# Windowed attention and channel mix: q and k of seven batches turned on VectorE instead of TensorE

## The chip, the cores and the metric

One core of a Trainium2 chip runs the whole program. Its engines run side by side, each through its own list of instructions in order: PE (TensorE: matmuls, and PEld for the weight loads), DVE (VectorE), ACT (ScalarE), POOL (GpSimd, which here mainly issues the loads) and SP (SyncE, which issues the stores). They wait for each other by semaphores. The metric is the device time of one execution in microseconds; the kernel before takes 245.48 us, the median of 3 runs from 244.85 to 245.68.

## The reference

```python
B, H, S, D = 8, 8, 576, 64                       # attention
scores = (q @ k.T) / sqrt(D)
rel = pos[:, None] - pos[None, :]
bias = slopes[h] * -abs(rel)                     # slopes: 2 ** -(h + 1)
scores = where((rel >= 0) & (rel < 128), scores + bias, -1e9)
attn_out = softmax(scores) @ v                   # per batch and head
x = attn_out as (B, S, 512)                      # channel mix
x_prev = x shifted down by one token, zero first
xk = mu_k * x + (1 - mu_k) * x_prev
xr = mu_r * x + (1 - mu_r) * x_prev
out = sigmoid(xr @ w_r) * (relu(xk @ w_k) ** 2 @ w_v)
```

The weights are 512x1024, 1024x512 and 512x512. Inputs and the output are float32; the kernel computes in bf16 with float32 sums.

## The kernel before, in words

**Pairs and units.** The attention runs over 32 pairs: pair `it` is batch b = it // 4 and the two heads 2g and 2g+1 with g = it % 4. A token attends to at most 128 tokens up to itself, so its keys lie in its own block of 128 tokens or in the one before: 576 tokens are four blocks and a tail of 64. The channel mix runs over two batches at a time (P = 0 to 3, 1152 tokens), cut into units of 256, 384 or 512 tokens.

**One pair, in order.** POOL loads q and k with a cast to bf16 (`load_ql`, lines 105 to 109: four heads of one of q and k for the first 512 tokens, four tokens on each of 128 partitions) and the tail of 64 tokens apart (`load_tail`, line 100). DVE gathers two heads by token (`by_token`, line 126, tile `ct`); PE turns them with eight transposes by the identity (`qk_transp`, line 135), so that the 64 numbers of a head lie on partitions, as the contraction of the scores wants it; ACT copies the result out of PSUM (`qk_copy`, line 115). Once in a batch PE turns the tails (`tail_transp`, line 148) and DVE copies them (lines 154 and 155). PE computes the scores in two halves of six matmuls with 64 rows each, the two heads side by side in the array (`scores`, line 187); ACT takes the exponential (line 195); DVE multiplies with the mask that holds bias and window (line 200); PE multiplies with v (`av`, line 218), where a column of ones gives the sums; DVE divides (`norm`, lines 229 and 230); PE turns the result (`x_transp`, line 238); ACT copies it to `xt` (line 243), channels on partitions.

**Mixing.** `mix` computes on DVE dl = x - x_prev (line 263) and then xk = mu_k dl + x_prev and xr = mu_r dl + x_prev (line 270), each in one instruction with the factor of the channel.

**Channel mix.** For a unit PE computes xk @ w_k in eight parts (`mm1`, line 281), ACT takes the relu (line 287), DVE squares it (`square`, line 292, tile `kk`), PE computes xr @ w_r (`mm3`, line 300), ACT the gate (line 306), PE the product with w_v in two halves (`mm2`, line 315), DVE multiplies with the gate (`product`, line 321), and SP stores the result (line 324).

**What sets the order.** A table `ORDER` fixes every engine's list (PE, ACT, DVE, POOL), and `plan` issues the operations by it. Names in it are an operation with its indices: `score.4.0` is the first half of the scores of pair 4, `m1.0.256.3` part 3 of `mm1` in the unit of P = 0 that begins at token 256, `kk`, `m3`, `m2a`, `m2` and `oo` belong to the same units. PSUM is shared by rings: two double banks `sa` (scores and av), one bank `tp` (transposes) and three banks `mm`. A matmul into a ring waits until the reader of the bank's last content is done.

Of the kernel before, what the change touches and what calls it, by code (L numbers as in the profile page):

```python
# [16 lines left out]
def kernel(  # L17
# [12 lines left out]
    nc = tc.nc  # L30
# [31 lines left out]
    p_tp = ctx.enter_context(tc.tile_pool(name="p_tp", bufs=1, space=bass.MemoryType.PSUM))  # L62
    p_mm = ctx.enter_context(tc.tile_pool(name="p_mm", bufs=3, space=bass.MemoryType.PSUM))
# [4 lines left out]
    ldr = cst.tile([128, 2, NHW, 2, NF * D], FP32, name="ldr")  # L68
    qk_buf = [cst.tile([128, 2, SM], BF16, name=f"qk{i}") for i in range(NBUF)]
    vs_buf = [cst.tile([128, NF, H, W], BF16, name=f"vs{i}") for i in range(NLD)]  # L70
    ql_buf = [cst.tile([128, 2, 2, H // 2, NF * D], BF16, name=f"ql{i}") for i in range(2)]
    ts_buf = [cst.tile([128, H, D], BF16, name=f"ts{i}") for i in range(NLD)]
    at_buf = [cst.tile([128, 2 * 1024 + 64], BF16, name=f"at{i}") for i in range(NAT)]

    tt_buf = [cst.tile([128, G, 3, 64], BF16, name=f"tt{i}") for i in range(2)]
    tv_buf = [cst.tile([128, H, W], BF16, name=f"tv{i}") for i in range(NLD)]
    xt_buf = [cst.tile([128, NPO, 2 + S], BF16, name=f"xt{i}") for i in range(2)]
# [22 lines left out]
    def load_tail(b, i):  # L100
        nc.gpsimd.dma_start(
            out=ts_buf[b % NLD][64 * i:64 * i + 64],
            in_=(q, k)[i][b, :, SM:S, :].rearrange("h p d -> p h d"))
# [40 lines left out]
    def tail_transp(b):  # L144
        ts = ts_buf[b % NLD]
# [6 lines left out]
    def tail_copy(b):  # L152
        t4 = T.pop(("tt", b))[:, 0:128 * G].rearrange("p (g t c) -> p g t c", g=G, t=2)
        nc.vector.tensor_copy(out=tt_buf[b % 2][:, :, 2], in_=t4[:, :, 0])
        nc.vector.tensor_copy(out=tt_buf[b % 2][:, :, 0], in_=t4[:, :, 1])
# [10 lines left out]
    def scores(it, e):  # L166
        early = it < NEARLY
        b, g = divmod(it, G)
        qk, tt = qk_buf[it % NBUF], tt_buf[b % 2]
# [19 lines left out]

    def at_half(it, e):  # L190
# [3 lines left out]
    def expo(it, e):  # L194
        nc.scalar.activation(out=at_half(it, e), in_=T.pop(("sa", it, e)),  # L195
                             func=AF.Exp, scale=float(scale))
# [26 lines left out]
    def norm(it, t0, t1):  # L223
# [3 lines left out]
        if t0 == 0 or it < G:  # L227
            xu = T["xu", it, t0] = xup.tile([128, NJ, 2, D], BF16, tag="xu", name="xu")
# [5 lines left out]
    def x_transp(it, t0=0, t1=NJ):  # L234
        xu = T.pop(("xu", it, t0))
        tp = T["xt", it, 128 * t0] = p_tp.tile([128, 1024], BF16, tag="tp", name="tp")
# [4 lines left out]
    def x_copy(it, c0=0, c1=S):  # L241
        b, g = divmod(it, G)
        nc.scalar.copy(out=xt_buf[b % 2][:, g, 2 + c0:2 + c1], in_=T.pop(("xt", it, c0))[:, c0:c1])  # L243

    def x_scaled(it, c0, c1):
        if c0 == 0:
            T["xm", it] = mxp.tile([128, S], BF16, tag="xm", name="xm", bufs=3)
        nc.scalar.activation(out=T["xm", it][:, c0:c1], in_=xt_buf[0][:, it, 2 + c0:2 + c1],
                             func=AF.Identity, scale=mu_sb[:, it:it + 1])

    def mix(it, which, c0=0, c1=S):
        b, g = divmod(it, G)
        P, e = divmod(b, 2)
        xc, xp = xt_buf[b % 2][:, g, 2 + c0:2 + c1], xt_buf[b % 2][:, g, 1 + c0:1 + c1]
        scaled = it in XMUL
        if which == 0:
            if e == 0 and g == 0 and c0 == 0:
                T["xk", P] = mxp.tile([128, NPO, SP], BF16, tag="xk", name="xk")
                T["xr", P] = mxp.tile([128, NPO, SP], BF16, tag="xr", name="xr")
        if c0 == 0 and which == int(scaled):  # L260
            T["dl", it] = mxp.tile([128, S], BF16, tag="dl", name="dl", bufs=4)
        if which == int(scaled):
            nc.vector.tensor_tensor(out=T["dl", it][:, c0:c1], in0=xc, in1=xp, op=ALU.subtract)  # L263
        to = T["xk" if which == 0 else "xr", P][:, g, S * e + c0:S * e + c1]
        if scaled and which == 0:
            nc.vector.scalar_tensor_tensor(
                out=to, in0=xp, scalar=mu_sb[:, 2 * NPO + g:2 * NPO + g + 1],
                in1=T["xm", it][:, c0:c1], op0=ALU.mult, op1=ALU.add)
            return
        nc.vector.scalar_tensor_tensor(  # L270
            out=to, in0=T["dl", it][:, c0:c1],
            scalar=mu_sb[:, NPO * which + g:NPO * which + g + 1], in1=xp, op0=ALU.mult, op1=ALU.add)
# [17 lines left out]
    def square(P, c0, c1, fo):  # L290
        rl = T.pop(("rl", P, c0, fo))
        nc.vector.tensor_tensor(out=T["kk", P, c0][:, fo, 0:c1 - c0], in0=rl[:, 0:c1 - c0],  # L292
                                in1=rl[:, 0:c1 - c0], op=ALU.mult)
# [25 lines left out]
    def product(P, c):  # L319
# [4 lines left out]
        nc.sync.dma_start(out=of[SP * P + 128 * c:SP * P + 128 * c + 128, :], in_=ot)  # L324
# [12 lines left out]
    mu_sb = cst.tile([128, 3 * NPO], FP32, name="mu_sb")  # L337
# [59 lines left out]
    def clear_first():  # L397
        clear_batch(nc.gpsimd, 0)
        nc.gpsimd.memset(tt_buf[0][:, :, 1], 0.0)

    RINGS = {"sa": 2, "tp": 1, "mm": 3, "ct": 3, "xu": 3, "dl": 4, "xm": 3, "xk": 2, "rl": 3,
# [497 lines left out]
```

## Time and profile before

| what | us |
|---|---|
| median of 3 runs | 245.48 |
| span of the profiled execution | 243.3 |
| PE busy | 232.5 |
| DVE busy | 202.5 |
| ACT busy | 173.6 |
| POOL busy | 77.2 |

The profiled execution is known by its span, from its first instruction to its last; 2.2 us separate that from the median of the runs, and they are taken to lie around the span. Busy time of PE counts a matmul until its modelled end, which the next one overlaps, so what a group of matmuls takes is read from its start to the start of what follows. On DVE and ACT, too, an instruction that depends on nothing late starts some 0.08 to 0.1 us before the one ahead of it ends.

### The profile page before, as it was taken

What the parts mean: (1) busy time and instruction counts of PE and PEld (TensorE: products, weight loads), DVE (VectorE), ACT (ScalarE), POOL (GpSimd) and SP (SyncE); (2) the same over time, 40 slices, a digit from 0 to 9 for tenths busy, and PEclk for the clock granted to TensorE, in tenths of its full rate; (3) what the DMA queues carried; (4) which work ended last, traced back from release to release, by engine and by line L of the source; (5) the groups of instructions that cost most, each with busy time, mean ns of one, the idle gap of its engine ahead of it and who ended that gap; (6) DMA issues with size and microseconds to landing.
All of it is one profiled execution on the core that took longest, in us unless ns stands there. A gap on an engine that the chain in (4) does not pass through costs nothing.

```text
span 243.3 us, 5721 instructions
## 1 busy us (share of the span) xinstructions
PE 232.5 (96%) x2295; PEld 140.1 (58%) x2295; DVE 202.5 (83%) x448; ACT 173.6 (71%) x281; POOL 77.2 (32%) x115
## 2 busy tenths in 40 slices
PE   7499989999999999999999999999999999999993
PEld 2246776657766656557566575565565656545641
DVE  6388999999999999998989989988779876883333
ACT  6378799979999896986977768878854666307700
POOL 8999485486272825100980000000000000000000
PEclk9999999999999999999999999999999999999999
DMA  7999999999997999921999120110201300132023
GB/s 135 160 155 191 158 174 205 167 185 223 193 150 95 153 194 108 167 52 46 96 174 212 51 89 0 46 46 0 86 34 55 132 1 1 46 129 86 0 89 131
DMA packets 70748, 26.86 MB, mean 110 GB/s; under 512 B 47161, under 2 KB 66113, under 8 KB 70721
## 3 DMA queue, kind: packets, MB, share of 16 engines
q0 software_dynamic: 64976, 16.52, 77.3%
q1 hardware_dynamic: 5744, 9.97, 11.3%
q8 instruction: 18, 0.29, 0.5%
q14 instruction: 10, 0.07, 0.1%
HBM read 33.56 MB, written 9.44 MB: 177 GB/s over the span
## 4 chain that ended last, share of the span: by engine, by line
PE 85%; DVE 8%; DMA 3%; POOL 1%; issue 1%; ACT 1%; POOLq 0%; DVEq 0%
PE pv L315 26%; PE ps L281 24%; PE pr L300 13%; PE sa L187 6%; PE sa L218 6%; PE tp L135 5%; PE tp L238 4%; DMA ql<-in_k_dram 3%; DVE xu L230 2%; DVE xk L270 1%; DVE xr L270 1%; DVE ct L126 1%; DVE kk L292 1%; DVE dl L263 1%; PE to L148 1%
## 5 line engine op out<-in xcount | busy, mean ns | idle before, releaser
L195 ACT ACTIVATE at<-sa 128x1024 bf16<-128x1024 f32 x64 | 65.4, 1037 | 12.1 <-PE sa L187 11.9
L281 PE MATMUL ps<-xk,wk_sb 128*128 128x256 bf16 (+2 forms) x416 | 73.2, 314 | 0.6 <-DVE xk L270 0.6
L315 PE MATMUL pv<-wv_sb,kk 128*128 128x512 bf16 x288 | 69.4, 379 | 0.0
L287 ACT ACTIVATE rl<-ps 128x256 bf16<-128x256 f32 (+2 forms) x104 | 46.9, 475 | 20.8 <-PE ps L281 16.6
L281 PEld LDWEIGHTS <-wk_sb 128*128 128x128 bf16 x416 | 38.2, 98 | 21.5 <-issue 1.3
L292 DVE TENSOR_TENSOR kk<-rl 128x256 bf16<-128x256 bf16 (+2 forms) x104 | 32.7, 335 | 12.9 <-ACT rl L287 12.6
L315 PEld LDWEIGHTS <-kk 128*128 128x128 bf16 x288 | 26.7, 98 | 27.5 <-issue 0.8
L115 ACT COPY qk<-tp 128x1024 bf16<-128x1024 bf16 (+1 forms) x32 | 31.0, 969 | 9.1 <-PE tp L135 5.1
L200 DVE TENSOR_TENSOR at<-at,mask 128x1024 bf16<-128x1024 bf16 x56 | 37.3, 683 | 0.0
L300 PE MATMUL pr<-wr_sb,xr 128*128 128x512 bf16 x144 | 36.0, 379 | 0.0
L87 POOL DMA_DIRECT2D vs<-in_v_dram x32 | 28.5, 905 | 22.5 <-PE sa L218 18.0
L321 DVE SCALAR_TENSOR_TENSOR ot<-rs,pv 128x512 f32<-128x512 bf16 x36 | 24.6, 683 | 11.8 <-PE pv L315 11.6
L270 DVE SCALAR_TENSOR_TENSOR xk<-dl,mu_sb,xt 128x576 bf16<-128x576 bf16 (+2 forms) x36 | 27.1, 752 | 1.3
L243 ACT COPY xt<-tp 128x576 bf16<-128x576 bf16 (+2 forms) x36 | 21.3, 591 | 8.8 <-PE tp L238 8.7
L306 ACT ACTIVATE rs<-pr 128x512 bf16<-128x512 f32 x36 | 22.1, 618 | 5.6 <-PE pr L300 5.5
L270 DVE SCALAR_TENSOR_TENSOR xr<-dl,mu_sb,xt 128x576 bf16<-128x576 bf16 x32 | 25.8, 810 | 0.0
L218 PEld LDWEIGHTS <-at 128*128 128x128 bf16 x576 | 21.6, 98 | 4.7 <-ACT at L195 0.3
L230 DVE TENSOR_TENSOR xu<-sa,rc 128x640 bf16<-128x640 f32 x28 | 23.1, 824 | 1.0
L135 PE MATMUL tp<-ident,ct 128*128 128x128 bf16 x248 | 19.0, 219 | 4.0 <-DVE ct L126 4.0
L135 PEld LDWEIGHTS <-ct 128*128 128x128 bf16 x248 | 15.5, 98 | 8.7 <-DVE ct L126 5.1
L300 PEld LDWEIGHTS <-xr 128*128 128x128 bf16 x144 | 13.3, 98 | 12.1
L187 PE MATMUL sa<-qk 64*128 64x256 bf16 (+1 forms) x256 | 19.8, 259 | 0.4 <-ACT at L195 0.3
(63 smaller groups left out, 215.6 us busy)
## 6 DMA issues: line engine op xcount, KB each, us to landing
out_dram<-ot SPq DMA_DIRECT2D x36, 256.0 KB, 2.0
vs<-in_v_dram POOLq DMA_DIRECT2D x32, 128.0 KB, 7.2
ql<-in_q_dram POOLq DMA_DIRECT2D x15, 256.0 KB, 7.7
ql<-in_k_dram POOLq DMA_DIRECT2D x15, 256.0 KB, 8.2
wk_sb<-in_moe_w_k_dram POOLq DMA_DIRECT2D x2, 512.0 KB, 7.9
wv_sb<-in_moe_w_v_dram POOLq DMA_DIRECT2D x2, 512.0 KB, 10.7
ts<-in_q_dram POOLq DMA_DIRECT2D x8, 64.0 KB, 7.3
ts<-in_k_dram POOLq DMA_DIRECT2D x8, 64.0 KB, 6.3
```

Of the source, the lines that this page charges most:

```text
L115: nc.scalar.copy(out=dst, in_=src)
L135: nc.tensor.transpose(tp[:, 128 * (n - NF * t0):128 * (n - NF * t0) + 128], cs[:, n // NF, n % NF].rearrange("p h d -> p (h d)"), ident)
L187: nc.tensor.matmul(sa[:, hl, c0:c0 + n], lhsT=kk_, rhs=qq_, start=not early, stop=True, skip_group_check=True)
L195: nc.scalar.activation(out=at_half(it, e), in_=T.pop(("sa", it, e)), func=AF.Exp, scale=float(scale))
L200: nc.vector.tensor_tensor(out=at_half(it, e), in0=at_half(it, e), in1=mask[:, 2 * g:2 * g + 2, 256 * e:256 * e + 512], op=ALU.mult)
L218: nc.tensor.matmul(pa[:, hl, W * (t - t0):W * (t - t0) + W], lhsT=at[:, lo:lo + 128], rhs=vs[:, u, 2 * g + hl, :] if u < NF else tvb[:, 2 ...
L270: nc.vector.scalar_tensor_tensor(out=to, in0=T["dl", it][:, c0:c1], scalar=mu_sb[:, NPO * which + g:NPO * which + g + 1], in1=xp, op0=ALU. ...
L281: nc.tensor.matmul(ps[:, 0:c1 - c0], lhsT=wk_sb[:, po, 128 * fo:128 * fo + 128], rhs=xk[:, po, c0:c1], start=(po == 0), stop=(po == NPO - 1))
L287: nc.scalar.activation(out=rl[:, 0:c1 - c0], in_=T.pop(("ps", P, c0, fo))[:, 0:c1 - c0], func=AF.Relu, scale=RELU_SCALE)
L292: nc.vector.tensor_tensor(out=T["kk", P, c0][:, fo, 0:c1 - c0], in0=rl[:, 0:c1 - c0], in1=rl[:, 0:c1 - c0], op=ALU.mult)
L300: nc.tensor.matmul(pr, lhsT=T["xr", P][:, po, 128 * c:128 * c + 128], rhs=wr_sb[:, po], start=(po == 0), stop=(po == NPO - 1))
L315: nc.tensor.matmul(pv, lhsT=kk[:, fo, o:o + 128], rhs=wv_sb[:, fo], start=(fo == 0), stop=(fo == NFO - 1))
```

## The change

**q and k of batches 1 to 7.** DVE now turns the loaded tiles itself: `turn` reads four heads of q or k as 32-bit words, each a pair of bf16, and transposes every 32x32 block of words. A block of 128 tokens is on 32 partitions with four tokens each, and stays there: word d of a head then lies on partition 32 u + d for block u, tokens along the row. `turn_tail` does it for the tails, which are loaded to 32 partitions with two tokens each. A block's queries meet the keys of the block before them, which lie 32 partitions lower, so `shift` copies three quarters of q by a DMA from SP to the columns behind. `scores4` contracts 32 words for the even and 32 for the odd numbers of a pair: per head 4 blocks x 2 parities, each with 32 rows of the array and a PSUM bank of its own, and two matmuls for the tail: 20 matmuls for a pair in place of 12. It needs both `sa` buffers at once. Batch 0 keeps the old way, in buffers that lie in tiles of later use.

**Mixing.** `mix` no longer forms dl. For xk, and again for xr, it multiplies x with mu and with 1 - mu into a buffer `mb` of four, and adds the second shifted by a token.

**mu through a turn.** `mu_copy` fills a tile with words whose upper halves are zero and lower halves 1.0, turns it, and scales mu with the 1.0 that comes out.

**Squares.** Those that the table lists under ACT run there: 67 of 104 (33 of 256 tokens, 20 of 384, 14 of 512).

**Around it.** One PSUM ring `mm` of four banks in place of `tp` and `mm`; stores are operations of their own, so that SP has a list too; loads of q and k are released by the turn; `ORDER` is a new table on all engines.

```diff
+    def words(ap, c):
+        return ap.rearrange("p h c t -> p (h c t)").bitcast(FP32).rearrange("p (h c) -> p h c", c=c)
+
+    def turn(b, w, i):
+        hs = slice(w * H // 2, (w + 1) * H // 2)
+        dst = words(kt_buf[b % 2], 128)[:, hs] if i else words(q2_buf[b % 2], 256)[:, hs, 0:128]
+        nc.vector.transpose(
+            dst.rearrange("p h (c r) -> p h r c", r=NF),
+            ql_buf[b % 2][:, w, i].rearrange("p h c -> p (h c)").bitcast(FP32).rearrange(
+                "p (h r d) -> p h r d", r=NF, d=32))
...
+    def shift(b, w):
+        hs = slice(w * H // 2, (w + 1) * H // 2)
+        qt = words(q2_buf[b % 2], 256)[:, hs]
+        nc.sync.dma_start(out=qt[0:96, :, 128:256], in_=qt[32:128, :, 0:128])
...
+    def scores4(it):
...
+            for par in range(2):
+                for u in range(NF):
+                    r, n = 32 * u, 256 if u < NF - 1 else 192
+                    nc.tensor.matmul(
+                        T["sa", it, u // 2][:, u % 2, 256 * hl:256 * hl + n],
+                        lhsT=kt[r:r + 32, h, :, par], rhs=qt[r:r + 32, h, 0:n, par],
+                        start=(par == 0), stop=(par == 1), skip_group_check=True)
+            for par in range(2):
+                nc.tensor.matmul(
+                    T["sa", it, 1][:, 1, 256 * hl + 192:256 * hl + 256],
+                    lhsT=kl[96:128, h, :, par], rhs=qt[96:128, h, 128:192, par],
+                    start=(par == 0), stop=(par == 1), skip_group_check=True)
...
     def mix(it, which, c0=0, c1=S):
-            nc.vector.tensor_tensor(out=T["dl", it][:, c0:c1], in0=xc, in1=xp, op=ALU.subtract)
-        nc.vector.scalar_tensor_tensor(
-            out=to, in0=T["dl", it][:, c0:c1],
-            scalar=mu_sb[:, NPO * which + g:NPO * which + g + 1], in1=xp, op0=ALU.mult, op1=ALU.add)
+        for i in range(2):
+            m = NPO * (2 * i + which) + g
+            nc.vector.tensor_scalar(out=mb[:, 1 - i, 2 + c0:2 + c1], in0=xc,
+                                    scalar1=mu_sb[:, m:m + 1], scalar2=None, op0=ALU.mult)
+        nc.vector.tensor_tensor(
+            out=T["xk" if which == 0 else "xr", P][:, g, S * e + c0:S * e + c1],
+            in0=mb[:, 1, 2 + c0:2 + c1], in1=mb[:, 0, 1 + c0:1 + c1], op=ALU.add)
...
     def square(P, c0, c1, fo):
+        if (P, c0, fo) in ACT_SQ:
+            nc.scalar.activation(out=out_, in_=in_, func=AF.Square)
+        else:
+            nc.vector.tensor_tensor(out=out_, in0=in_, in1=in_, op=ALU.mult)
...
     def mu_copy():
+        nc.vector.memset(one_in[:, :, 0], 1.0)
+        nc.vector.memset(one_in[:, :, 1], 0.0)
+        nc.vector.transpose(one_out.rearrange("p c t -> p (c t)").bitcast(FP32),
+                            one_in.rearrange("p c t -> p (c t)").bitcast(FP32))
+        nc.vector.tensor_copy(out=one, in_=one_out[:, 0:1, 0])
+        nc.vector.tensor_scalar(out=mu_sb[:, 0:2 * NPO], in0=T.pop("mu")[:, 0:2 * NPO],
+                                scalar1=one, scalar2=None, op0=ALU.mult)
...
     ORDER = {
+            pk.1 cmu tcopy.0 tl.1.0 norm.0.0 pk.2 norm.1.0 tr.1.0.0 xk.0.0 tr.1.0.1
+            lq.0.0 lq.0.1 lmu.0 lmu.1 sh.1.0 sh.1.1 sh.2.0 st.0.0 st.0.1 st.0.2 sh.2.1
```

**Where the order moves: DVE, between the first results of batch 0 and the mixing that follows.** Before, with `ct` the gathered q and k, `dl` and `xk` the mixing, `kk` a square, `rc` and `xu` the division:

```order
L229 RECIPROCAL rc<-pa 128x2x3
L230 TENSOR_TENSOR xu<-pa,rc 128x2x3x64
L126 COPY ct<-ql_94 128x1024
L292 TENSOR_TENSOR kk<-rl 128x256
L126 COPY ct<-ql_94 128x1024
L263 TENSOR_TENSOR dl<-xt_107 128x320
L270 SCALAR_TENSOR_TENSOR xk<-dl,mu_sb,xt_107 128x320
```

In the change, with `qt` and `kt` the turned q and k and `mb` the products with mu and 1 - mu:

```order
L176 STREAM_TRANSPOSE qt_90<-ql_80 128x4x4x32
L290 RECIPROCAL rc<-pa 128x2x3
L291 TENSOR_TENSOR xu<-pa,rc 128x2x3x64
L315 TENSOR_SCALAR mb_100<-xt_94,mu_sb 128x320 x2
L317 TENSOR_TENSOR xk_96<-mb_100 128x320
L315 TENSOR_SCALAR mb_102<-xt_94,mu_sb 128x320 x2
L317 TENSOR_TENSOR xk_96<-mb_102 128x320
L315 TENSOR_SCALAR mb_100<-xt_94,mu_sb 128x256 x2
L317 TENSOR_TENSOR xk_96<-mb_100 128x256
L315 TENSOR_SCALAR mb_102<-xt_94,mu_sb 128x256 x2
L317 TENSOR_TENSOR xk_96<-mb_102 128x256
L176 STREAM_TRANSPOSE kt_86<-ql_80 128x4x4x32
```

The gathers are gone, turns for batch 1 stand between the divisions and the mixing of batch 0, a mixed output is three rows in place of two, and the squares of the first units are no longer in this list.

**SP's list.** Before, with `ldr` the first loads and `ot` the results:

```order
L81 DMA ldr<-in_q_dram 128x2x256
L81 DMA ldr<-in_k_dram 128x2x256
L630 DMA mu_row<-in_moe_mu_k_dram 4x128
L630 DMA mu_row<-in_moe_mu_r_dram 4x128
L324 DMA out_dram<-ot 128x512 x36
```

In the change, from the fifth row on, with the shifts of q within `qt`:

```order
L192 DMA qt_90<-qt_90 96x4x128 x2
L192 DMA qt_89<-qt_89 96x4x128
L377 DMA out_dram<-ot 128x512 x3
L192 DMA qt_89<-qt_89 96x4x128
L377 DMA out_dram<-ot 128x512
L192 DMA qt_90<-qt_90 96x4x128 x2
L377 DMA out_dram<-ot 128x512
```

Shifts for a batch stand among the stores of results that are computed a batch or more earlier; a shift waits behind the stores ahead of it, and a store behind the shifts.

500 lines of the change are left out of this document (271 added, 229 removed).

## The prediction

> **What bounds the kernel now.** I read the head of the page first, then the chain of waits, then PE's waits.
>
> ```profile
> span 243.3 us, 5721 instructions
> PE 232.5 (96%) x2295; PEld 140.1 (58%) x2295; DVE 202.5 (83%) x448; ACT 173.6 (71%) x281; POOL 77.2 (32%) x115
> ...
> PE pv L315 26%; PE ps L281 24%; PE pr L300 13%; PE sa L187 6%; PE sa L218 6%; PE tp L135 5%; PE tp L238 4%; DMA ql<-in_k_dram 3%; DVE xu L230 2%; DVE xk L270 1%; DVE xr L270 1%; DVE ct L126 1%; DVE kk L292 1%; DVE dl L263 1%; PE to L148 1%
> ```
>
> PE is busy nearly throughout, and the chain runs on it but for the start. L135, the transposes that the change takes away, is 5% of the chain, 12 us. Next PE's waits (total us, count, longest), then four stretches (start:end, length, busy time of PE, PEld, DVE, ACT, POOL, granted clock, DMA share, GB/s):
>
> ```profile
> PE tp L135 <- DVE ct L126: 4.0, 3, 2.0
> PE wm L160 <- DVE zero L387: 1.2, 1, 1.2
> ...
> 0.00:24.00 24.00, 18.58 (x207) 9.81 (x208) 16.23 (x54) 15.46 (x26) 22.64 (x46) 1.00 1.46 160
> 24.00:45.00 21.00, 19.41 (x233) 14.29 (x231) 20.69 (x56) 18.89 (x34) 11.75 (x16) 1.00 1.90 181
> 45.00:165.00 120.00, 120.00 (x1321) 74.77 (x1319) 114.14 (x237) 99.89 (x151) 42.83 (x55) 1.00 1.08 120
> 165.00:243.30 78.30, 74.55 (x541) 41.28 (x539) 51.43 (x104) 39.40 (x71) 0.00 (x0) 1.00 0.16 61
> ```
>
> PE waits on DVE only in the first two stretches; from 45 to 165 us it is never idle, at the full clock. DVE is nearly as full there (114 of 120). So I need two sums: PE's rows, and DVE's ahead of what PE waits for.
>
> **Prices of PE.** From start to start of successive groups, since the modelled ends overlap:
>
> ```profile
> 45.71 0.39 PE L187 MATMUL sa<-qk 64*128 64x256 bf16 x4
> ...
> 47.36 0.62 PE L218 MATMUL sa<-vs,at 128*128 128x65 bf16 x15
> 47.91 1.02 PE L315 MATMUL pv<-wv_sb,kk 128*128 128x512 bf16 x4
> ...
> 151.92 0.56 PE L187 MATMUL sa<-qk 64*128 64x256 bf16 x8
> ...
> 152.47 1.04 PE L281 MATMUL ps<-xk,wk_sb 128*128 128x512 bf16 x4
> 153.34 0.61 PE L135 MATMUL tp<-ident,ct 128*128 128x128 bf16 x8
> 153.79 1.03 PE L300 MATMUL pr<-wr_sb,xr 128*128 128x512 bf16 x4
> 154.65 1.03 PE L315 MATMUL pv<-wv_sb,kk 128*128 128x512 bf16 x4
> ...
> 166.20 0.56 PE L187 MATMUL sa<-qk 64*128 64x256 bf16 x8
> ```
>
> Eight transposes take 0.45 us (153.34 to 153.79), a tail's four half of that, the scores of a pair 0.55 (151.92 to 152.47), four matmuls of 512 columns 0.86 (153.79 to 154.65), thus 0.42 ns a column; the av of a pair 0.55, about 30 ns for each matmul with its weights.
>
> The 20 new matmuls with 32 rows are in no row. If four row groups always run beside each other, 4096 columns become 1024, 0.43 us a pair; if they run one after another, 1.73. The nearest row for many small matmuls, each with weights of its own, is av: 20 x 30 ns = 0.60, which I take. The Trainium skill ("TensorE: Matmul & The Clock Gate", Part 3: Packing small matmuls) has four 32-row groups measured at 3.07 times the serial speed; 1.73 / 3.07 = 0.56 us, an estimate, and the sum would be 1.1 us lower. No run here shows it yet.
>
> PE's list: 28 x 0.45 = 12.6 and seven tails, 1.6, go; 28 x 0.05 = 1.4 comes. Net -12.8 us.
>
> **Prices of DVE.** The groups by form (busy, mean ns of one | idle before), and one tile's first, middle and longest duration:
>
> ```profile
> L126 DVE COPY ct<-ql 128x1024 bf16<-128x1024 bf16 x31 | 13.5, 445 | 4.5 <-DMA ql<-in_k_dram 4.5
> L112 DVE COPY qk<-tp 128x512 bf16<-128x512 bf16 x4 | 2.7, 686 | 1.4 <-PE tp L135 0.7 <-ACT qk L115 0.7
> L112 DVE CAST cs<-ldr 128x512 bf16<-128x512 f32 x2 | 0.8, 417 | 0.0
> L292 DVE TENSOR_TENSOR kk<-rl 128x256 bf16<-128x256 bf16 x48 | 12.7, 284 | 7.0 <-ACT rl L287 6.8
> L292 DVE TENSOR_TENSOR kk<-rl 128x512 bf16<-128x512 bf16 x24 | 9.9, 417 | 0.2 <-ACT rl L287 0.2
> ...
> L126 DVE COPY ct<-ql x31: 414/420/672, 6.9 to 165.8; 128x1024 bf16<-128x1024 bf16 x31
> ...
> L361 DVE TENSOR_SCALAR sid<-ident x8: 174/212/476, 2.5 to 3.2; 128x128 bf16<-128x128 bf16 x8
> ```
>
> Where nothing is waited for, a row starts about 0.08 us before the end of the one ahead, so the price in a full list is the duration less 0.08.
>
> A turn moves 512 words of 32 bits per partition. Below, the CAST, which reads 512 such words: 0.417 - 0.08 = 0.34. The COPY with 512 elements at 686 ns, the slow kind: 0.61. Above, twice the element part of that, as the turn writes every fourth word: 0.08 + 2 x 0.53 = 1.14. I take 0.60: the turn reads and writes 32-bit words, which the CAST does on one side alone. 42 turns are 25.2 us. They replace 28 copies of 0.335 (9.4) and 14 tail copies of 0.20 (2.8; row below).
>
> The rest of a pair on DVE, which stays: the two halves of the mask, 0.60 each (0.683 - 0.08), and the division, 0.74 and some 0.25 with its small reciprocal (the last row is the tail copy):
>
> ```profile
> L200 DVE TENSOR_TENSOR at<-at,mask 128x1024 bf16<-128x1024 bf16 x56 | 37.3, 683 | 0.0
> L230 DVE TENSOR_TENSOR xu<-sa,rc 128x640 bf16<-128x640 f32 x28 | 23.1, 824 | 1.0
> ...
> L154 DVE COPY tt<-to 128x256 bf16<-128x256 bf16 x8 | 2.3, 285 | 0.3 <-PE to L148 0.2
> ```
>
> Mixing before is three rows for two outputs:
>
> ```profile
> 24.05 0.28 DVE L263 TENSOR_TENSOR dl<-xt 128x256 bf16<-128x256 bf16 x1
> ...
> 69.22 0.45 DVE L263 TENSOR_TENSOR dl<-xt 128x576 bf16<-128x576 bf16 x1
> 69.70 0.82 DVE L270 SCALAR_TENSOR_TENSOR xk<-dl,mu_sb,xt 128x576 bf16<-128x576 bf16 x1
> 70.44 0.81 DVE L270 SCALAR_TENSOR_TENSOR xr<-dl,mu_sb,xt 128x576 bf16<-128x576 bf16 x1
> 71.17 0.45 DVE L263 TENSOR_TENSOR dl<-xt 128x576 bf16<-128x576 bf16 x1
> ```
>
> That is 1.95 us for 576 tokens (69.22 to 71.17). The new multiply lies between `sid` (128 elements, 212 ns) and `ct` (1024, 420): 0.232 ns an element, 316 ns at 576, 0.22 in the list. If it ran at the rate of `kk` (0.52 ns an element from 256 to 512): 450 ns, 0.37. The addition is like `kk`, 0.37, plus 0.12 since it waits for the second product to its end. An output is 2 x 0.22 + 0.37 + 0.12 = 0.93, a pair 1.86; over the list 3.0 us less. The 67 squares on ACT take 33 x 0.20 + 20 x 0.27 + 14 x 0.34 = 17 us (rounded shapes included) off DVE; the scaling of mu adds 0.7. Sum for DVE: -9.4 - 2.8 - 17.0 - 3.0 + 25.2 + 0.7 = -6.3.
>
> A rule speaks against all this. The Trainium skill ("SBUF — State Buffer", SBUF: two separate sides) says that DVE's fast two-port modes and GpSimd lock each other out of a shared port for whole instructions. The rows bear a little of it out: the longest of the 31 gathers took 672 against 420 ns, the mean is 25 ns over the middle, and POOL issues most of the time up to 165 us. On 106 multiplies ahead of the scores of pair 28 that is 2.7 us.
>
> **ACT.** The 28 copies go and the squares come, at relu's price, which has the same shapes:
>
> ```profile
> L115 ACT COPY qk<-tp 128x1024 bf16<-128x1024 bf16 x28 | 28.7, 1024 | 3.9 <-PE tp L135 3.4
> L287 ACT ACTIVATE rl<-ps 128x256 bf16<-128x256 f32 x48 | 17.7, 395 | 5.2 <-PE ps L281 3.4 <-issue 1.2 <-DVE kk L292 0.4
> L287 ACT ACTIVATE rl<-ps 128x512 bf16<-128x512 f32 x24 | 14.6, 607 | 4.3 <-PE ps L281 2.5 <-DVE kk L292 1.6
> ```
>
> In the list a copy is 0.90, 25.2 in all; a square 0.31, 0.41 or 0.52 (the row less 0.09), 25.8. ACT stays where it is, at 100 of 120 us in the full stretch, and hides this.
>
> **The sum by stages.** I cut at PE's scores of pair 8 (before at 45.71) and of pair 28 (166.20).
>
> First stage: PE's rows ahead of the cut are 31.5 us before, so it is 14.2 late; in the change 33.5, for parts of `mm2` are moved ahead of it: 47.7 if PE sets it. But these scores need the turned tail `tl.2.1`. DVE's rows up to it: start and batch 0's turning 8.1, 12 divisions 9.0, 16 mixed outputs 12.3, eight masks 4.8, ten turns 6.0: 40.2. Before, the row at 24.05 has 13.9 us of rows ahead of it, so DVE loses 10.1 us at its start, and is full afterwards (20.69 of 21.00). I keep these 10.1: 50.3 us. DVE sets the first cut, 4.6 later than before.
>
> Second stage: PE's rows were 116.5 and took 120.5 (166.20 - 45.71), a factor of 1.034. In the change they are 104.7: 21 x 0.45 = 9.4 and five tails, 1.1, fall away, scores add 1.0, rows of units moved elsewhere take 2.3. 104.7 x 1.034 = 108.3. DVE has 110.0 us of rows up to the first mask of pair 28 and then stands at 10.1 + 40.2 + 110 = 160.3, against 158.6 for PE's scores of that pair: abreast, with 1.7 us between them, which 8 us of other matmuls between those scores and their av cover.
>
> The new wait in this stage: the scores need both `sa` buffers, and everything on PE queues behind them. What frees these is two exponentials after the scores of another pair, or a division after its av:
>
> ```profile
> PE sa L187 <- ACT at L195: 0.3, 1, 0.3
> ...
> L195 ACT ACTIVATE at<-sa 128x1024 bf16<-128x1024 f32 x64 | 65.4, 1037 | 12.1 <-PE sa L187 11.9
> ```
>
> The two take 1.8 us, the division 1.0. Between the two rows in PE's list stand matmuls of 1.3 to 6 us, at nine of 20 places under 2.2. That covers it if ACT or DVE is free at that moment; a mask (0.60) or a relu (0.3 to 0.5) ahead makes PE wait some 0.5. Below nothing, above 9 x 0.5 = 4.5; I take a quarter, 1.2, as both engines have gaps elsewhere but DVE hardly any.
>
> Third stage: before 243.26 - 166.20 = 77.1, rows 72.5. In the change 69.6 of rows (two groups of transposes and two units' parts fewer): 74.2.
>
> 50.3 + 108.3 + 1.2 + 74.2 = 234.0 for the span, against 243.3. With the 2.2 us that the median (245.48) has over the profiled execution: **236.2 us**. Of PE's 12.8, 2.6 are lost at the first cut to DVE.
>
> **Rivals.** *PE sets everything.* If the start on DVE loses less than 10.1 us, the first cut is at 47.7, and without the wait for `sa` it gives 47.7 + 108.3 + 74.2 + 2.2 = 232.4; with 0.43 a pair, 28 x 0.17 = 4.8 less: 227.6. For it: DVE is busy in only 16.23 of the first 24 us, so turns could go into its gaps. Against: DVE is full from 24 us on.
>
> *Turns or multiplies cost more: slower.* At 1.14 a turn, 42 x 0.54 = 22.7 us stand on DVE, all ahead of pair 28's masks, where it has nothing to spare: 258.9. From (245.5 - 236.2) / 42 = 0.22 above my price (0.82 us) the kernel is slower than before. Multiplies at 0.37 make 2 x 0.15 on each of 53 outputs, 15.9: 252.1. For it: no row shows a transpose on DVE, nor a multiply by a column at this length. Against: `sid` at 212 ns is on the fast line.
>
> *The 32-row matmuls do not run beside each other*, so the change is not what it says: 28 x 1.13 = 31.6, 267.8; from 0.93 us a pair it is slower. Against: before, two 64-row matmuls of 256 columns take 0.55 / 6 = 0.09 us together, less than 2 x 0.108.
>
> *Ports.* The lock-out of the skill's rule as `ct` bears it out: 2.7 us on DVE, 238.9.
>
> *Transfers at the start.* A shift takes what a store takes, and stands in one queue with them:
>
> ```profile
> out_dram<-ot SPq DMA_DIRECT2D x36, 256.0 KB, 2.0
> ```
>
> In order with stores of earlier units it lands about 2 us after its turn. If the first two each hold PE up that long: 240.2. Against: a batch is 30 us.
>
> **How the numbers follow.** Forecast with sizes as priced 0.57 (own range 231 to 241), ports 0.05, PE alone 0.11, turns or multiplies slower 0.17, serial scores 0.07, start 0.03. The runs can tell about 0.3%, 0.7 us, from no change. The slower rivals have intermediate sizes, some of them near 245: faster 0.72, same 0.04, slower 0.24. The range 230 to 252 leaves out the serial scores, the full price of a turn, and the lowest PE case, some 0.2.
>
> **What would show it.** The turn's mean near 0.68 us and the multiply's near 0.32 in the groups by form; the first scores of pair 8 about 50 us, with PE's waits ahead of it put down to DVE; of pair 28 at 158 to 161; 0.6 us from the scores to what follows. Wrong is the forecast if PE shows waits on the turn, mixing or masks after 50 us (DVE became the bound), if waits name ACT's square, or if the scores take over 0.9 us.

## The result: slower, with DVE as the bound

The changed kernel takes 261.29 us (median of 4 runs, 260.8 to 261.88) against 245.58 before on the same chip (244.85 to 246.22): a ratio of 1.065, interval 1.062 to 1.068. The forecast was 236.2. Times here and below are medians of the executions within 1.5% of the kernel's fastest.

The chain's shares by engine before; then, after, the head of the page, the chain's shares by engine and by line, and the longest of PE's waits (total us, count, longest):

```profile
PE 85%; DVE 8%; DMA 3%; POOL 1%; issue 1%; ACT 1%; POOLq 0%; DVEq 0%
```

```profile
span 259.0 us, 5730 instructions
PE 225.4 (87%) x2234; PEld 132.2 (51%) x2267; DVE 217.2 (84%) x485; ACT 171.8 (66%) x320; POOL 76.2 (29%) x118
...
DVE 51%; PE 34%; DMA 5%; issue 5%; ACT 3%; DVEq 0%; ACTq 0%
PE ps L328 11%; DVE mb L315 10%; PE pv L365 9%; DVE at L262 9%; PE pr L350 6%; DVE xu L291 6%; DVE ot L371 5%; DVE qt L176 4%; DVE kt L176 4%; DMA qt<-qt 3%; DVE xr L317 3%; PE wm L197 3%; DVE xk L317 3%; DMA out_dram<-ot 2%; ACT at L258 2%
...
PE sa L237 <- DVE xr L317: 6.6, 1, 6.6
PE sa L237 <- DMA qt<-qt: 4.0, 2, 3.6
PE xp L299 <- DVE xu L291: 2.9, 4, 1.3
```

The chain ran 85% on PE before and runs 51% on DVE now. PE lost work, as meant (232.5 to 225.4 us busy), and is not busy in 33.6 us of the span. DVE, which the forecast had at 6.3 us less, is 14.7 us busier. The multiplies of the mixing (`mb`, L315) lead its lines in the chain with 10%; the mask has 9%, the turns of q and k (L176) together 8%.

The stretches, cut near PE's scores of pair 8 and pair 28 (start:end, length, busy time of PE, PEld, DVE, ACT, POOL, granted clock, DMA share, GB/s):

```profile
0.00:24.00 24.00, 19.65 (x204) 10.51 (x207) 20.03 (x59) 15.09 (x26) 22.83 (x49) 1.00 1.35 161
24.00:45.00 21.00, 11.42 (x146) 8.56 (x143) 15.82 (x41) 12.89 (x27) 11.32 (x15) 0.76 1.59 183
45.00:58.00 13.00, 12.43 (x145) 7.95 (x145) 12.32 (x28) 10.07 (x25) 1.48 (x2) 1.00 1.35 129
58.00:184.00 126.00, 112.26 (x1240) 66.48 (x1259) 121.43 (x243) 94.42 (x165) 40.54 (x53) 0.99 0.91 116
184.00:259.00 75.00, 69.62 (x521) 38.66 (x518) 47.58 (x117) 39.39 (x78) 0.00 (x0) 1.00 0.20 74
```

Two things went wrong in two places. From 58 to 184 us DVE is full (121.4 of 126) and PE is not (112.3). From 24 to 45 both have holes: something else held them. The two cuts themselves (start, length, ..., idle before and its releaser), and the rows of DVE that stand there, the last tail turn of batch 2 and the first mask of pair 28:

```profile
57.71 0.41 PE L237 MATMUL sa<-qt,kt 32*128 32x256 bf16 x8 [0.41 <-DMA qt<-qt]
...
183.65 0.41 PE L237 MATMUL sa<-qt,kt 32*128 32x256 bf16 x8
...
58.04 0.70 DVE L184 STREAM_TRANSPOSE kl<-kl 32x512 f32<-32x512 f32 x1
...
187.46 0.68 DVE L262 TENSOR_TENSOR at<-at,mask 128x1024 bf16<-128x1024 bf16 x1
```

| stage | forecast | measured |
|---|---|---|
| to the scores of pair 8 | 50.3 | 57.7 |
| from there to pair 28 | 109.5 | 125.9 |
| to the end | 74.2 | 75.4 |
| span | 234.0 | 259.0 |

The last stage came nearly as forecast, 1.2 us longer. The 25 us are 7.4 in the first and 16.4 in the second. (The scores of pair 8 begin at 57.71, but their matmuls on the tail wait for the tail turn until 58.81.) What DVE's new rows cost, in the groups by form (busy, mean ns of one | idle before):

```profile
L315 DVE TENSOR_SCALAR mb<-xt,mu_sb 128x576 bf16<-128x576 bf16 x120 | 40.7, 381 | 3.2 <-ACT xt L304 2.9
L317 DVE TENSOR_TENSOR xr<-mb 128x576 bf16<-128x576 bf16 x32 | 14.7, 459 | 1.2
L176 DVE STREAM_TRANSPOSE kt<-ql 128x512 f32<-128x512 f32 x14 | 15.4, 1099 | 0.0
L176 DVE STREAM_TRANSPOSE qt<-ql 128x512 f32<-128x512 f32 x14 | 15.3, 1090 | 0.0
L184 DVE STREAM_TRANSPOSE qt<-kl 32x512 f32<-32x512 f32 x7 | 4.9, 706 | 0.2
```

And in its timeline, from start to start:

```profile
98.87 0.64 DVE L315 TENSOR_SCALAR mb<-xt,mu_sb 128x576 bf16<-128x576 bf16 x2
99.55 0.46 DVE L317 TENSOR_TENSOR xr<-mb 128x576 bf16<-128x576 bf16 x1
99.92 0.64 DVE L315 TENSOR_SCALAR mb<-xt,mu_sb 128x576 bf16<-128x576 bf16 x2
100.60 0.46 DVE L317 TENSOR_TENSOR xr<-mb 128x576 bf16<-128x576 bf16 x1
100.98 1.10 DVE L176 STREAM_TRANSPOSE kt<-ql 128x512 f32<-128x512 f32 x1
101.93 0.67 DVE L262 TENSOR_TENSOR at<-at,mask 128x1024 bf16<-128x1024 bf16 x1
```

A turn is 0.95 us (100.98 to 101.93; forecast 0.60), a mixed output 1.05 (98.87 to 99.92; forecast 0.93). A tail turn, 706 ns, is near its price.

The hole from 24 to 45 us, at the scores of pair 7 and at the second shift, which they need:

```profile
26.30 0.59 SPq L192 DMA_DIRECT2D qt<-qt  x1
...
37.38 0.61 PE L237 MATMUL sa<-qt,kt 32*128 32x256 bf16 x8 [6.63 <-DVE xr L317]
```

The wait is put down to a mixing row, but that row had no part in these scores. In the trace the shift issued at 26.30 landed 10.9 us later, at 37.24. Of all shifts, and by median against the stores in the same queue:

```profile
DMA to landing us min/median/max: 2.7/5.0/10.9
...
out_dram<-ot SPq DMA_DIRECT2D x36, 256.0 KB, 2.6
...
qt<-qt SPq DMA_DIRECT2D x14, 192.0 KB, 5.0
```

So there are three suspects: the turn's price, the price of the mixing, and the landing of the shift.

### The profile page after: what moved, and what is told of

It reads as the page before. It is cut to its first block, busy times and chain, and to the rows that moved or that the text cites. A ratio compares the mean times of both kernels' runs of the same rounds, so it can differ in the third digit from the quotient of the medians.

```text
span 259.0 us, 5730 instructions
## 1 busy us (share of the span) xinstructions
PE 225.4 (87%) x2234; PEld 132.2 (51%) x2267; DVE 217.2 (84%) x485; ACT 171.8 (66%) x320; POOL 76.2 (29%) x118
## 4 chain that ended last, share of the span: by engine, by line
DVE 51%; PE 34%; DMA 5%; issue 5%; ACT 3%; DVEq 0%; ACTq 0%
PE ps L328 11%; DVE mb L315 10%; PE pv L365 9%; DVE at L262 9%; PE pr L350 6%; DVE xu L291 6%; DVE ot L371 5%; DVE qt L176 4%; DVE kt L176 4%; DMA qt<-qt 3%; DVE xr L317 3%; PE wm L197 3%; DVE xk L317 3%; DMA out_dram<-ot 2%; ACT at L258 2%
## 5 line engine op out<-in xcount | busy, mean ns | idle before, releaser
L328 PE MATMUL ps<-xk,wk_sb 128*128 128x256 bf16 (+2 forms) x412 | 74.4, 317 | 4.5 <-DVE xk L317 2.5
L365 PE MATMUL pv<-wv_sb,kk 128*128 128x512 bf16 x274 | 67.2, 379 | 1.8 <-DVE ot L371 0.8
L315 DVE TENSOR_SCALAR mb<-xt,mu_sb 128x576 bf16<-128x576 bf16 (+2 forms) x136 | 45.3, 379 | 3.2 <-ACT xt L304 2.9
L341 ACT ACTIVATE kk<-rl 128x256 bf16<-128x256 bf16 (+2 forms) x67 | 32.2, 500 | 0.2
L237 PE MATMUL sa<-qt,kt 32*128 32x256 bf16 x448 | 20.1, 271 | 13.7 <-DVE xr L317 6.6
L356 ACT ACTIVATE rs<-pr 128x512 bf16<-128x512 f32 x36 | 21.7, 611 | 10.5 <-PE pr L350 10.2
L304 ACT COPY xt<-xp 128x576 bf16<-128x576 bf16 (+2 forms) x36 | 20.8, 591 | 7.8 <-PE xp L299 7.5
L237 PEld LDWEIGHTS <-kt 32*128 32x128 bf16 x448 | 10.6, 93 | 24.2 <-issue 9.5
L280 PE MATMUL sa<-vs,at 128*128 128x65 bf16 x448 | 18.9, 194 | 1.2 <-DVE at L262 1.1
L343 DVE TENSOR_TENSOR kk<-rl 128x256 bf16<-128x256 bf16 (+2 forms) x37 | 12.0, 343 | 9.4 <-ACT rl L334 9.4
L120 POOL DMA_DIRECT2D ql<-in_q_dram x15 | 11.7, 778 | 22.7 <-DVE qt L176 18.7
```

Source lines behind the costliest of these rows:

```text
L237: nc.tensor.matmul(T["sa", it, u // 2][:, u % 2, 256 * hl:256 * hl + n], lhsT=kt[r:r + 32, h, :, par], rhs=qt[r:r + 32, h, 0:n, par], star ...
L280: nc.tensor.matmul(pa[:, hl, W * (t - t0):W * (t - t0) + W], lhsT=at[:, lo:lo + 128], rhs=vs[:, u, 2 * g + hl, :] if u < NF else tvb[:, 2 ...
L315: nc.vector.tensor_scalar(out=mb[:, 1 - i, 2 + c0:2 + c1], in0=xc, scalar1=mu_sb[:, m:m + 1], scalar2=None, op0=ALU.mult)
L328: nc.tensor.matmul(ps[:, 0:c1 - c0], lhsT=wk_sb[:, po, 128 * fo:128 * fo + 128], rhs=xk[:, po, c0:c1], start=(po == 0), stop=(po == NPO - 1))
L341: nc.scalar.activation(out=out_, in_=in_, func=AF.Square)
L365: nc.tensor.matmul(pv, lhsT=kk[:, fo, o:o + 128], rhs=wv_sb[:, fo], start=(fo == 0), stop=(fo == NFO - 1))
```

## The experiments

Each kernel ran beside the kernel before on the same chip. On these chips the kernel before took 244.9 to 245.6 us, so a difference between two kernels that ran on different chips is good to some 0.7 us. Differences are to the change's 261.29 unless said otherwise. Lines left out of a diff are marked by dots.

**e1: turns that write in a row.**

```diff
-        dst.rearrange("p h (c r) -> p h r c", r=NF)
+        dst.rearrange("p h (r c) -> p h r c", r=NF)
```

> The 28 turns write their words in a row instead of every fourth word; the tokens of a block then stand in another order, so the attention is not the reference's. All else as in the change (261.3 us). If the step of 16 bytes in the write is what makes a turn 0.95 us from start to start, the turn falls to about 0.62, as forecast, and since DVE sets the end the time falls by 28 x 0.33 = 9 us, to some 252. If the transpose itself costs 0.95, turn and time stay: 261 within 1.

249.96 us, ratio 1.021 (1.016 to 1.026) to before: 11.3 us less than the change. The turn's group:

```profile
L176 DVE STREAM_TRANSPOSE kt<-ql 128x512 f32<-128x512 f32 x14 | 9.8, 702 | 0.0
```

1099 ns became 702. DVE is 10.2 us less busy (207.0), and the time follows it a little further. Of it 10.1 us come off the second stage (125.9 to 115.8), 0.8 off the first. The step of the write is the excess of the turn, and DVE sets the second stage.

**e2: no shifts.**

```diff
-        qt = words(q2_buf[b % 2], 256)[:, hs]
-        nc.sync.dma_start(out=qt[0:96, :, 128:256], in_=qt[32:128, :, 0:128])
+        pass
...
+        nc.gpsimd.memset(q2_buf[1][0:96, :, 128:256], 0.0)
```

> The 14 shifts of q are left out (the columns behind hold zeros or old numbers, so the scores against the block before are not computed). If DVE's work bounds the kernel and a late shift only holds PE up at the scores of pair 7 (6.6 us) and twice later (4.0 us), most of that is eaten by DVE behind it: 255 to 258 us. If the landing of the shifts (3 to 11 us) is the main loss, the whole 10.6 us and more come back: 250 or less. If nothing hangs on them, 261.

254.45 us, ratio 1.040 (1.034 to 1.045): 6.8 us less, a little below the first range. The scores of pair 8 start at 54.26 in place of 57.71, which is 3.4 of the 4.8 us between the two profiled spans (254.2 and 259.0); DVE stays as busy as in the change (217.0) and is 61% of the chain. So the late shift costs mainly in the first stage, and the larger part of the loss is not the shift's.

**e3: mixing as before.** (`xp` is `xt` read one column earlier, and `dl` lies in `mb`.)

```diff
...
-        for i in range(2):
-            m = NPO * (2 * i + which) + g
-            nc.vector.tensor_scalar(out=mb[:, 1 - i, 2 + c0:2 + c1], in0=xc,
-                                    scalar1=mu_sb[:, m:m + 1], scalar2=None, op0=ALU.mult)
-        nc.vector.tensor_tensor(
-            out=T["xk" if which == 0 else "xr", P][:, g, S * e + c0:S * e + c1],
-            in0=mb[:, 1, 2 + c0:2 + c1], in1=mb[:, 0, 1 + c0:1 + c1], op=ALU.add)
+        if which == 0:
+            nc.vector.tensor_tensor(out=dl, in0=xc, in1=xp, op=ALU.subtract)
+        nc.vector.scalar_tensor_tensor(
+            out=T["xk" if which == 0 else "xr", P][:, g, S * e + c0:S * e + c1], in0=dl,
+            scalar=mu_sb[:, NPO * which + g:NPO * which + g + 1], in1=xp, op0=ALU.mult, op1=ALU.add)
```

> Mixing as before the change (difference, then one instruction for xk and one for xr); all else as in the change. By the trace of the change an output now costs 0.28 + 0.40 + 0.38 = 1.06 us on DVE, a pair 2.12, against 1.95 before, and more where POOL works. If DVE bounds the kernel, some 26 pairs ahead of the end of the second stage give 26 x 0.17 = 4.4 us back or a little more: 255 to 257. If shifts or the buffers of the scores bound it, 261 within 1.

253.42 us, ratio 1.034 (1.029 to 1.039): 7.9 us less, more than the 4.4 that the quiet rows of the timeline gave. DVE's busy time fell by 7.3 (209.9): in the change the 74 multiplies of the second stage take 391 ns on the mean, while POOL issues loads, and those of the last stage 366; in e3 the old rows for xk take 819 ns with and without an instruction of POOL beside them.

**e4: prices by themselves.** Blocks of five on DVE behind everything else, with PE and POOL at rest:

```diff
+    wa = ql_buf[0][:, 0, 0].rearrange("p h c -> p (h c)").bitcast(FP32)
+    wo = kt_buf[0].rearrange("p h c t -> p (h c t)").bitcast(FP32)[:, 0:512]
...
+    for _ in range(R):
+        nc.vector.transpose(wo.rearrange("p (h c r) -> p h r c", c=32, r=4), wa.rearrange("p (h r d) -> p h r d", r=4, d=32))
+    for _ in range(R):
+        nc.vector.transpose(wo.rearrange("p (h r c) -> p h r c", c=32, r=4), wa.rearrange("p (h r d) -> p h r d", r=4, d=32))
+    for _ in range(R):
+        nc.vector.transpose(wo.rearrange("p (h r c) -> p h r c", c=32, r=4), wa.rearrange("p (h d r) -> p h r d", r=4, d=32))
...
+    for _ in range(R):
+        nc.vector.tensor_scalar(out=mb[:, 1, 0:S], in0=xc, scalar1=mu_sb[:, 0:1], scalar2=None, op0=ALU.mult)
+    for _ in range(R):
+        nc.vector.tensor_scalar(out=mb[:, 1, 0:S], in0=xc, scalar1=0.5, scalar2=None, op0=ALU.mult)
```

> The change with blocks of five instructions added on DVE behind everything else, where POOL and PE rest: the turn as it is; with a write in a row; with a read at a step and a write in a row; on 32 partitions; with a write of every second word; plain copies of the same words, in a row and with the step of four; the multiply of 576 numbers at the offset of the change, at none, with a constant in place of the column, and as a copy. If the step of the write costs, the second block is near 0.6 us and the first near 0.95, and the stepped copy is dearer than the plain one; if the transpose costs by its partitions, the 32-partition block is near 0.6 and the others 0.95. If the multiply is slow for its offset or its column, the blocks without them are faster than 0.28 us from start to start; if not, all are alike.

```profile
L967 DVE STREAM_TRANSPOSE kt<-ql 128x512 f32<-128x512 f32 x5 | 5.4, 1080 | 0.2
L963 DVE STREAM_TRANSPOSE kt<-ql 128x512 f32<-128x512 f32 x5 | 5.4, 1076 | 0.1
L969 DVE STREAM_TRANSPOSE kt<-ql 32x512 f32<-32x512 f32 x5 | 5.3, 1068 | 0.2
L971 DVE STREAM_TRANSPOSE kt<-ql 128x512 f32<-128x512 f32 x5 | 3.6, 712 | 0.2
L965 DVE STREAM_TRANSPOSE kt<-ql 128x512 f32<-128x512 f32 x5 | 3.6, 712 | 0.2
L975 DVE COPY kt<-ql 128x512 f32<-128x512 f32 x5 | 3.1, 620 | 0.2
L973 DVE COPY kt<-ql 128x512 f32<-128x512 f32 x5 | 2.1, 427 | 0.2
L980 DVE TENSOR_SCALAR mb<-xt,mu_sb 128x576 bf16<-128x576 bf16 x5 | 1.9, 372 | 0.2
L978 DVE TENSOR_SCALAR mb<-xt,mu_sb 128x576 bf16<-128x576 bf16 x5 | 1.8, 367 | 0.1
L984 DVE COPY mb<-xt 128x576 bf16<-128x576 bf16 x5 | 1.6, 312 | 0.2
L982 DVE TENSOR_SCALAR mb<-xt 128x576 bf16<-128x576 bf16 x5 | 1.6, 311 | 0.2
```

The three transposes of the diff are L963, L965 and L967, its two multiplies L980 and L982. A step of four words costs a turn 0.36 to 0.37 us, in the write (L963) as in the read (L967), and on 32 partitions (L969) as on 128. A step of two words in the write (L971) costs as little as none (L965), which is why the tail turns with their step of two came near their price. A copy pays for the step too (620 against 427). The multiply costs 55 to 60 ns more by a column than by a constant or as a copy; its offset does not matter (L978, L980).

**e5: all three edits at once.**

> The first three edits together: turns that write in a row, mixing as before the change, no shifts (leaves out the scores against the block before and the order of the tokens in a block). Alone they gave 11.3, 6.8 and 7.9 us off 261.3. If the forecast was right but for these three costs (turn, multiply, landing of the shift), their sum comes back and the time is near the forecast's 236: 234 to 238. If something else holds the kernel as well (the buffers of the scores, ACT with its squares), it stops earlier, at 241 or more. If PE alone sets it then, its rows give 230 to 233.

239.38 us, ratio 0.976 (0.972 to 0.979), between the first two ranges. Its two cuts, and its longest wait of PE:

```profile
50.38 0.40 PE L236 MATMUL sa<-qt,kt 32*128 32x256 bf16 x8
...
163.28 0.40 PE L236 MATMUL sa<-qt,kt 32*128 32x256 bf16 x8
...
PE ps L326 <- DVE xk L315: 2.2, 2, 1.7
```

Without the three costs the stages are 50.4, 112.9 and 74.0 (237.3 - 163.28) against the forecast's 50.3, 109.5 and 74.2. The first and the last are within 0.2 us of the forecast; 3.4 us remain in the second. This kernel leaves part of the attention out and is no version to use.

**e6: turns in a row and old mixing, shifts kept.**

> Turns that write in a row and mixing as before, shifts as in the change. If both only take work off DVE and DVE is the bound, 11.3 + 7.9 come off: 242. If the shifts become the next wait (8.4 us of PE's waits with the cheap turns, 10.1 with the old mixing), part is given back: 243 to 246. Before took 245.2, so this also says whether a turn with the price that was forecast would have paid.

248.49 us, ratio 1.012 (1.009 to 1.016), above both ranges. The two edits gave 11.3 and 7.9 alone, but 12.8 together, and dropping the shifts on top gives 9.1 more. PE's first wait says why:

```profile
PE sa L237 <- DMA qt<-qt: 9.0, 3, 5.5
```

Once DVE is relieved the shift is the next bound: from e6 to e5 the first stage falls from 57.0 to 50.4 us and the second from 115.9 to 112.9. So a turn at the forecast's price would not have paid either, with these shifts.

**e7: squares back on DVE.**

```diff
-    ACT_SQ = {tuple(map(int, w.split(".")[1:])) for w in ORDER.get("ACT", "").split()
-              if w.startswith("kk.")}
+    ACT_SQ = set()
...
+        line = [o for o in line if o[0] != "kk"]
```

> All 104 squares on DVE, as before the change, at the places that the plan finds; all else as in the change. 17 us of DVE's work come back, some 14 of it ahead of the scores of pair 28. If DVE bounds the second stage, the time grows by 10 to 15: 271 to 276. If ACT with its squares was what held PE, the time falls under 260. If PE or the shifts bound it, 261 to 264.

271.99 us, ratio 1.108 (1.098 to 1.117): 10.7 us more, with DVE 17.0 busier (234.2), and the second stage is 132.8 in place of 125.9. The same bound from the other side; and the squares on ACT are the part of the change that earned what it was given.

**e8: shifts in fewer, longer runs.**

```diff
...
-    q2_buf = [cst.tile([128, H, 256, 2], BF16, name=f"qt{i}") for i in range(2)]
+    q2_buf = [cst.tile([128, 2, H, 128, 2], BF16, name=f"qt{i}") for i in range(2)]
...
-        nc.sync.dma_start(out=qt[0:96, :, 128:256], in_=qt[32:128, :, 0:128])
+        nc.sync.dma_start(out=qt[0:96, 1, hs].rearrange("p h c t -> p (h c t)"),
+                          in_=qt[32:128, 0, hs].rearrange("p h c t -> p (h c t)"))
...
-                        lhsT=kt[r:r + 32, h, :, par], rhs=qt[r:r + 32, h, 0:n, par],
+                        lhsT=kt[r:r + 32, h, :, par], rhs=qt[r:r + 32, :, h, :, par],
```

> The columns behind q lie in a half of the tile of their own, so that a shift is 96 runs of 2 KB in place of 384 of 512 bytes; the scores of the last block read 256 columns in place of 192, and the tail's overwrite the rest. All else as in the change (261.3). If a shift lands late because of its number of runs among the packets of the loads, the median landing falls from 5.0 us to 3 or less, the long one at 26 us from 10.9 to 4, and the time comes near that without shifts (254.5): 254 to 257. If it waits for the bytes ahead of it whatever its form, landing and time stay: 260 to 262.

258.01 us, ratio 1.055 (1.050 to 1.061): 3.3 us less, or some 2.4 by the ratios (1.065 to 1.055), as this chip was a little faster.

```profile
DMA to landing us min/median/max: 2.5/4.6/8.3
```

Neither expectation holds: with a quarter as many runs the median landing falls by 8%. The longest falls from 10.9 to 8.3, which says little: with shifts of the old form it is 8.4 in e1, 8.9 in e3 and 10.2 in e6. Most of the landing time is not the number of runs.

**e9: a complete version with q turned in a row.** The mask has its queries in the turned order, and the transposes behind av restore it; k keeps its step of four, since its columns must be in the order of v's rows. Old mixing, shifts as in e8.

```diff
...
+            dst = words(q2_buf[b % 2][:, 0], 128)[:, hs].rearrange("p h (r c) -> p h r c", r=NF)
...
-                tp[:, 128 * t:128 * t + 128], xu[:, t].rearrange("p h d -> p (h d)"), ident)
+                tp[:, 128 * t:128 * t + 128], xu[:, t].rearrange("p h d -> p (h d)"),
+                ident if it < G or t == NF else identp)
```

> A version that computes all: q turned with a write in a row (the mask has its queries in that order, and the transposes behind av put the tokens back by an identity with permuted columns), k turned as in the change, mixing as before the change, shifts in 96 runs of 2 KB. DVE has 14 x 0.37 = 5.2 us less for q and what the old mixing gave, 7.9 us of time. If the short shifts land in time, 261.3 - 5 - 7.9 - 5 = 243, which is less than before (245.4); if they do not, 248 to 250.

251.06 us, ratio 1.023 (1.017 to 1.030), a little above the second range: the shifts do not land in time (they are 7.8 us of PE's waits).

**e10: the shift as copies on POOL**, in the version of e9.

```diff
...
-        nc.sync.dma_start(out=qt[0:96, 1, hs].rearrange("p h c t -> p (h c t)"),
-                          in_=qt[32:128, 0, hs].rearrange("p h c t -> p (h c t)"))
+        for r in range(0, 96, 32):
+            nc.gpsimd.tensor_copy(
+                out=qt[r:r + 32, 1, hs].rearrange("p h c t -> p (h c t)").bitcast(FP32),
+                in_=qt[r + 32:r + 64, 0, hs].rearrange("p h c t -> p (h c t)").bitcast(FP32))
```

> The version of the run before (q turned in a row, old mixing, 251.1 us), with each shift as three copies of 32 partitions on POOL in place of a DMA, placed among POOL's loads by the plan. If PE's waits for the shifts (7.8 us) were waits for DMAs queued behind the loads, a shift takes 2 to 3 us in place of 4.4 to 8 and 4 to 7 us come back: 244 to 247. If the turns that feed them were late, the waits are put down to the turn or the copy and the time stays: 250 to 252. If the copies hold the loads up or make DVE's instructions longer while they run, it grows: 253 or more.

250.32 us, ratio 1.023 (1.019 to 1.026): the same time, for other reasons than the range of 250 to 252 had. The wait for the shift has gone (0.7 us is left), the scores of pair 8 start at 51.1 in place of 57.9, but the copies are not free: from there to pair 28 are 122.4 us in place of 117.6. POOL's group, what PE still waits for in the shift, and two groups of DVE in e10, then one of the same in e9:

```profile
L195 POOL COPY qt<-qt 32x512 f32<-32x512 f32 x42 | 31.7, 756 | 50.1 <-DVE qt L181 38.8 <-DVE rc L295 9.4
...
PE sa L242 <- POOL qt L195: 0.7, 1, 0.7
...
L267 DVE TENSOR_TENSOR at<-at,mask 128x1024 bf16<-128x1024 bf16 x56 | 39.5, 728 | 0.0
L181 DVE STREAM_TRANSPOSE kt<-ql 128x512 f32<-128x512 f32 x14 | 15.4, 1100 | 0.0
```

```profile
L265 DVE TENSOR_TENSOR at<-at,mask 128x1024 bf16<-128x1024 bf16 x56 | 37.1, 684 | 5.6 <-ACT at L261 5.5
```

The mask went from 684 to 728 ns on the mean, and DVE as a whole from 205.6 to 211.2 us busy. By overlap in e10's trace, the ten masks beside a copy took 936 ns and the other 46 took 683; the one turn of k beside a copy took 1100 and the five tail turns 705, against 701 for the others. The Trainium skill ("SBUF — State Buffer", SBUF: two separate sides) says that a GpSimd instruction that reads SBUF and a DVE instruction with two SBUF inputs exclude each other at a shared port. The mask has two such inputs and the turn one, so the trace agrees, though few turns ran beside a copy.

No complete version that ran is faster than the kernel before. One with k in a row as well was not tried: its v would have to be loaded in another order.

## Why the prediction was wrong, point by point

The sum was of the right kind, and three of its terms were mis-sized: the turn, the mixing and the landing of the shift.

**What bounds the kernel before:** PE, with DVE nearly as full, was read rightly, and so was the danger in it: the forecast had the two abreast in the second stage, 1.7 us apart, so a higher price on DVE went into the time almost whole.

**The turn** is the step that failed first. The bounds were 0.34 and 1.14 us; the upper one was made for the right reason, "the turn writes every fourth word". I took 0.60 by the plain rows and kept the reason as a bound. It is 0.95: 28 x 0.35 = 9.8 us, of which 22 turns, 7.7, lie in the second stage. Without the step a turn is 0.63 from start to start in e5, so the plain rows gave the right price for another turn. By the slower rival the kernel loses from 0.82 us a turn on. It is the one that came, by its mechanism: e1 gave 11.3 back. That its sum at 1.14 us, 258.9, lies near the 261.3 measured is luck: the turn is cheaper than that, and mixing and shift make up the rest. The 14 tail turns measured 0.73 against 0.60, 1.8 us.

**The mixing** was the second. An output was to cost 0.93 and costs 1.05, 37 x 0.12 = 4.4 us in the second stage in quiet rows. My slope for the multiply came from a multiply by a constant and a copy, which e4 shows at 311 ns, close to the 316 that I had worked out; by a column it is 367. So the row was of another kind than the operation. "3.0 us less over the list" was a gain where e3 shows a loss of 7.9.

**DVE's second stage** then adds up: from the end of the last tail turn of batch 2 (58.78, where the next row starts) to the first mask of pair 28 (187.46) are 128.7 us, against 110.0 of forecast rows. 22 turns x 0.35, 10 tail turns x 0.13 and 37 outputs x 0.12 are 13.4 of those 18.7; one wait of 2.1 for ACT and 1.9 by which the 74 multiplies are longer than in the last stage make 17.4. That DVE, not PE, sets this stage is shown by its length between the same cuts: 125.9 us in the change, 115.8 in e1, 118.7 in e3, 132.8 in e7.

**The shift** was underrated as a rival of 0.03, with 2 us for a landing, from the stores' row. Its landing is 5.0 by median and 10.9 at the worst, at 26 us, while the loads are under way. The median hid this in the trace of before already, whose stores have

```profile
DMA to landing us min/median/max: 2.0/2.0/7.9
```

and whose first store, issued at 49.94, landed 5.7 us later. e2 prices it at 6.8 us in the change; when DVE is relieved it is 9.1 (e6 to e5). In the first stage it cost PE 6.6 us at the scores of pair 7, and then DVE, which had nothing to mask (two waits of 2.0 and 2.7 us for ACT). The first cut, 57.7 in the change, is at 56.9 in e1, 57.4 in e3, 54.3 in e2 and 50.4 with all three edits: there each cost hides behind the others.

**The 32-row matmuls** were priced rightly, 0.60 against 0.57:

```profile
42.21 0.40 PE L237 MATMUL sa<-qt,kt 32*128 32x256 bf16 x8
...
42.78 0.94 PE L328 MATMUL ps<-xk,wk_sb 128*128 128x256 bf16 x7
```

From 42.21 to 42.78 run the 20 matmuls of a pair, at the full clock. The Trainium skill's factor ("TensorE: Matmul & The Clock Gate", Part 3: Packing small matmuls) gave 0.56, and the trace agrees.

**The squares** on ACT and the **wait for both `sa` buffers**: ACT stayed at 171.8 us busy, as priced. PE waited 2.2 us for divisions ahead of its scores in the change, 0.3 in e5; 1.2 had been taken.

**Ports**: in the change the 49 multiplies during which POOL had an instruction take 418 ns on the mean, the other 87 take 357: 49 x 0.06 = 3.0 us, near the 2.7 of that rival, but as one part of the loss. The masks show no such difference (682 and 683 ns). No run took POOL's issues away, so that they are the cause is not shown.

**What stays open:** the 3.4 us of the second stage in e5, which has all three costs out. DVE is busy in 110.8 of its 112.9 us, and by rows most of it is still DVE's: from the end of the last tail turn of batch 2 (51.81) to the first mask of pair 28 (166.02) are 114.2 us against 110.0, of which 18.5 pairs of the old mixing (1.95 against 1.86) make 1.7, ten tail turns 1.3 and 22 turns at 0.63 another 0.7. No run tests that. Open is also how much of a shift's landing is bytes queued ahead of it, since e8 changed the runs alone.

## What to carry to other kernels

Price an operation by a row with the same access: the same step in words, and the same kind of scalar. Where no such row exists, and an end of the range has a reason in the code, take that end. If two engines stand abreast, work moved from the one to the other pays only where the other is relieved of more than arrives; add up both lists before looking at the one that is relieved. A DMA's landing is to be read from the stage in which it will run, with the loads of that stage, not from a quiet one.

## What the runs showed of the hardware

For a transpose of 128x512 words on DVE, a step of two 32-bit words in the write is free (712 ns), and a step of four, in the write or in the read, costs half as much again (1076 and 1080 ns). A column as the factor costs a fast multiply of 576 numbers 55 to 60 ns (367 and 372 against 311).

From 30.7 to 40.3 us of the change, over PE's stop of 6.6 us and nearly 3 us behind it, the granted clock was 0.50 (the last number but two of the row); it was 1.00 over the first 24 us and again from 42.2 on:

```profile
30.70:40.30 9.60, 2.96 (x31) 2.24 (x31) 7.50 (x20) 2.81 (x5) 5.74 (x8) 0.50 1.49 184
```

24 matmuls of 256 columns took from 38.35 to 42.21, 0.16 us each, where 256 columns at the 0.42 ns of the prediction's rows are 0.11. By this estimate the lower clock added some 1.3 us to the wait.

POOL's copies lengthened the DVE masks that ran beside them (683 to 936 ns), and left the five tail turns beside them nearly alone (701 to 705).
